# Attention scores in blocks of 64 by 64 in a fused attention and two-MLP kernel

## The chip, the cores and the metric

The kernel runs on one core of a Trainium2 chip. The metric is the device time of one execution in microseconds (us). Engines are named as in the profile: PE is TensorE's matrix multiply and PEld its weight loads, DVE is VectorE, ACT is ScalarE, POOL is GpSimd, and SP is the engine whose queue issues most DMA transfers.

## The reference, cut to what matters

Attention with decay over 2 batches, 8 heads, 768 positions and head dimension 64, in blocks of 64 positions, and then two MLPs on the 1536 rows of 512:

```python
for b in range(nb):                         # nb = 768 // 64 blocks
    intra = einsum('bhic,bhjc->bhij', qb, kb) * Dmask    # lam**(i-j) where i >= j, else 0
    intra = einsum('bhij,bhjd->bhid', intra, vb)
    inter = einsum('bhid,bhde->bhie', qb * lam_pow, kv_state)
    out[:, :, sl] = intra + inter
    kv_state = lam_block * kv_state + einsum('bhsd,bhse->bhde', kb * rev_pow, vb)
...
x = (h * cos(h)) @ w_out1      # h = x @ w_in1
y = (g * sigmoid(g)) @ w_out2  # g = x @ w_in2
```

Because the decay is a power of the distance, the kernel may use blocks of another length than 64: the result is the same.

## The kernel before, in words

All sequences of work are written out by hand: each engine runs its instructions in the order in which the program issues them, and waits on semaphores where its data come from another engine.

**Attention.** The kernel works in chunks of 128 positions, six of them (`SC = 6`), with both batches and all eight heads in one step. For a chunk it loads k, q and v (`load_qkv`, line 253, 512 KB each, on SP), transposes k and q on PE into PSUM (`transposed`, line 265, `pt`), and ACT copies the transposes to SBUF (`att_kT` line 269, `att_q` line 283). The PSUM tile of the k transposes and that of the q transposes share one buffer (tag "t", one buffer), so q's transposes wait until ACT has copied k's, and the next chunk's k transposes wait until ACT and DVE (`att_qdec`, line 291, `qd`) have read q's.

The scores of a chunk (`att_scores`, lines 335 to 344) are made in two calls, one per batch. A call has 8 products of 128 keys by 128 queries with a contraction of 64, two of which run at a time on the two row halves of the array. DVE then multiplies each of the two score tiles by the table `dm` of decay powers, in which the part above the diagonal is zero (line 344, 128 x 512). `att_inter` (line 357) adds the part from the running state: 16 products of 64 by 64 by 128, on the four quadrants of the array. `att_intra` (line 365) multiplies the masked scores by v: 16 products with a contraction of 128 keys, 64 output rows and 128 queries, on the two column halves. `att_kdec` and `att_kv` (lines 304 and 318) build the next state, `att_state` (lines 326 to 332) adds it to the decayed old one; the decay `sdec` of the new state is a POOL instruction (line 332). `att_x`, `att_t` and `att_l` (lines 377 to 410) turn the finished chunk into the operands of the first MLP: copies on ACT, differences `xt` on DVE (line 396), a rounding copy on ACT (line 408) and three subtractions on POOL (line 410), the third of which needs the copy of line 408.

**The order of a chunk.** Iteration `c` of the loop does `att_kv(c-1)`, `att_state(c-1)`, `att_scores(c-1, 0)`, `att_t(c-2)`, the k transposes of chunk `c`, `att_scores(c-1, 1)`, `att_kdec(c)`, `att_l(c-2)`, the q transposes of `c`, `att_inter(c-1)`, `att_qdec(c)`, `att_intra(c-1)`, `att_x(c-1)`. In iterations 3 and 4 there is also the preparation of the first weights of the MLP: `rebias_w` on ACT (line 112) before the copy of q's transposes, and `convert_w` on DVE (lines 121 and 122, `sb` and `w`) between `att_inter` and `att_qdec`. In iteration 5 there are also `sum_w` (line 143) and `split_plain` (lines 127 and 128).

**The start.** POOL makes the identity and the array `diag`. DVE makes the decay table by a scan along the free dimension (line 222, `dm<-step,diag`), a second scan makes the table `qp` (line 222). POOL copies one head's column of k and of q behind the last one (`head_17`, line 259), which the last transposes need.

**The end of the attention.** The last chunk's scores, `att_inter` and `att_intra` stand after the loop, between the first products of the first MLP (`product`, line 444). The MLP stages that follow (lines 440 to 750) are not touched.

Of the kernel before, what the change touches and what calls it, by code (L numbers as in the profile page):

```python
# [8 lines left out]
F32 = mybir.dt.float32  # L9
# [4 lines left out]
ALU = mybir.AluOpType  # L14
PSUM = bass.MemoryType.PSUM

P = 128
WARM = 4
TB = 512
HB = TB // 2  # L20
C = 64
# [19 lines left out]
def tile_decay_attention__two_mlps(  # L41
# [171 lines left out]
    def place(b, h):  # L213
        return (h - b) % H // 2, (h + b) % 2

    ident = ap_c.tile([P, P], F32, name="ident")
    lamb = ap_c.tile([P, P], F32, name="lamb")[:, 0:H + 1]
    dm = ap_c.tile([P, H + 1, P], F32, name="dm")
    qp = ap_c.tile([P, B, NP, P], F32, name="qp")

    def scan(out, step, first):
        nc.vector.tensor_tensor_scan(out=out, data0=step, data1=first, initial=0.0, op0=ALU.mult, op1=ALU.add)

    def table_dm():
        step = stage.tile([P, H, P], F32, tag="raw", name="step")
        nc.vector.tensor_copy(step, lamb[:, 0:H, None].to_broadcast([P, H, P]))
        nc.vector.memset(step[:, :, 0:1], 0.0)
        scan(*(t.rearrange("p h i -> p (h i)") for t in (dm[:, 0:H], step, diag)))
        nc.vector.tensor_copy(dm[:, H], dm[:, 0])

    def table_qp():
        first, step = both[:, 0], both[:, 1]
# [10 lines left out]
    def load_qkv(c, parts="kqv", engine=None):  # L243
        if c >= SC:
            return
        r = slice(c * P, (c + 1) * P)
        for part in parts:
            pool = ap_2 if part == "v" else ap_k
            t = pool.tile([P, 2 * H if part == "v" else 2 * H + 2, D], F32, tag=part, name=part, bufs=2 if part == "q" else 3)
            x = {"q": q, "k": k, "v": v}[part].rearrange("b h s d -> s (b h) d")[r]  # L250
            eng = engine or nc.sync
            for h in (slice(0, H), slice(H, 2 * H)) if c == 0 else (slice(0, 2 * H),):
                eng.dma_start(out=t[:, h], in_=x[:, h])
            qkv[c, part] = t
# [44 lines left out]
    def att_kdec(c):  # L299
        if c == SC - 1:  # L300
            return
        t = ap_k.tile([P, B, H, D], F32, tag="kd", name="kd", bufs=1)
        for b in range(B):
            (nc.gpsimd if c else nc.vector).tensor_tensor(
                out=t[:, b], in0=qkv[c, "k"][:, b * H:(b + 1) * H], in1=dm[:, 0:H, P - 1:P].to_broadcast([P, H, D]), op=ALU.mult
            )
        kd[c] = t

# [12 lines left out]
    def att_state(c):  # L321
        if c == SC - 1:
            return
        new = ap_2.tile([P, B, NP, D], F32, tag="state", name="state")
        if c:
            nc.vector.tensor_tensor(out=new, in0=pkv.pop(c), in1=sdec.pop(c), op=ALU.add)
        else:
            nc.vector.tensor_copy(new, pkv.pop(c))
        state[c + 1] = new
        if c < SC - 2:  # L330
            t = ap_2.tile([P, B, NP, D], F32, tag="sdec", name="sdec", bufs=1)
            nc.gpsimd.tensor_tensor(out=t, in0=new, in1=qp[:, :, :, P - 1:P].to_broadcast([P, B, NP, D]), op=ALU.mult)
            sdec[c + 1] = t

    def att_scores(c, b, pool, tag):
        (qT, _), kT = tr[c, "q"], tr[c, "k"]
        if b == 0:
            at[c] = ap_2.tile([P, B, 2, NP, P], F32, tag="at", name="at", bufs=1)
        ps = [pool.tile([P, NP, P], F32, tag=tag, name="psc", bufs=3) for _ in range(2)]
        for s in range(NP):  # L340
            for r in range(2):
                nc.tensor.matmul(ps[r][:, s, :], kT[half[r], b, s, :], qT[half[r], b, s, :], start=True, stop=True)  # L342
        for r in range(2):
            nc.vector.tensor_tensor(out=at[c][:, b, r], in0=ps[r], in1=dm[:, b + r:b + r + H - 1:2, :], op=ALU.mult)

    def att_inter(c, pool, tag):
        ps = pool.tile([P, B, NP, P], F32, tag=tag, name="pso")
# [5 lines left out]
        for s in range(NP):  # L353
            for e in range(2):
                for b in range(B):
                    u, r = place(b, 2 * s + e)
                    nc.tensor.matmul(ps[half[e], b, s, :], st[half[r], b, u, :], qd[half[r], b, u, :], start=s == 0, stop=False, skip_group_check=True)  # L357

    def att_intra(c):
        ps, a, vt = po[c], at.pop(c), qkv[c, "v"]  # L360
        for b in range(B):
            for s in range(NP):
                for e in range(2):
                    u, r = place(b, 2 * s + e)
                    nc.tensor.matmul(  # L365
                        ps[half[e], b, s, :], vt[:, b * H + 2 * s + e, :], a[:, b, r, u, :],
                        start=c == 0 and s == 0, stop=True, skip_group_check=True,
                    )

    def att_x(c):  # L370
# [473 lines left out]
    with tc.manual_schedule():  # L844
# [22 lines left out]
        nc.gpsimd.tensor_copy(diag, ident[:, None, :].to_broadcast([P, H, P]))  # L867
        both = ap_2.tile([P, 2, B, NP, P], F32, tag="at", name="both", bufs=1)
        nc.gpsimd.memset(both[:, 0], 0.0)
        nc.gpsimd.memset(both[:, 1, :, :, 0:1], 0.0)  # L870
        table_dm()

        for c in range(SC):
            if c == 0:
                pt = ps_t.tile([P, B, NP, P], F32, tag="t", name="pt")
                transposed(c, "k", pt, 0)
                warm(WARM)
                for part in "kq":
                    head_17(c, part, nc.gpsimd.tensor_copy)
                transposed(c, "k", pt, 1)  # L880
                att_kdec(c)
                table_qp()
                att_kT(c, pt)
                warm(WARM // 2)
                load_qkv(c + 2, "k")
                att_q(c, ps_o, "o")
                load_qkv(c + 2, "qv")
                head_17(c + 1, "k", nc.scalar.copy)
                continue
# [183 lines left out]
```

## Time and profile before

| what | value |
|---|---|
| median of 3 runs | 561.61 us (561.52 to 562.08) |
| time of the profiled execution | 561.36 us |
| its span in the trace | 559.5 us |
| PE busy | 553.3 us, 99% of the span |
| DVE, ACT, POOL busy | 357.4, 296.7, 185.2 us |
| chain that ended last | PE 96%, DVE 2%, DMA 1% |

Times inside the trace count from the start of the span. The profiled execution's own time is 1.86 us longer than its span, and 0.25 us below the median of the runs. A busy PE is not a PE at its peak, since matmuls are pipelined; what a piece of work costs on PE is read from the start of one group of matmuls to the start of the next.

### The profile page before, as it was taken

The numbers are of one execution on the slowest core, as the hardware profiler recorded it, in microseconds if no ns is written. First come the engines' busy times: TensorE is split into PE (matmuls) and PEld (weight loads), VectorE is DVE, ScalarE is ACT, GpSimd is POOL, SyncE is SP. The second block draws the span as 40 slices with busy tenths as digits, with TensorE's granted clock in tenths as the row PEclk, the third lists the DMA queues.
The fourth block names the chain that finished last, engine by engine and source line by source line (L and its number), as shares of the span: only waits on it lengthen the run. The fifth ranks groups of instructions, "written<-read, shape, count | busy, mean of one in ns | idle before, by whom it ended". The sixth has DMA issues, their size and how long they took to land.

```text
span 559.5 us, 8256 instructions
## 1 busy us (share of the span) xinstructions
PE 553.3 (99%) x3170; PEld 462.1 (83%) x3170; DVE 357.4 (64%) x452; ACT 296.7 (53%) x452; POOL 185.2 (33%) x162
## 2 busy tenths in 40 slices
PE   8999999999999999999999999999999999999997
PEld 5888788888888888888888898888888888888885
DVE  6697887777899976301896375666777966104322
ACT  5667577777788765202843575656656753101210
POOL 4699244444453000001552265555514000000000
PEclk9999999999999999999999999999999999999999
DMA  9994325554449988501322054455669993005501
GB/s 211 261 252 146 116 110 189 187 183 180 158 187 353 327 310 296 189 0 39 113 77 75 0 221 157 171 188 189 225 233 315 364 327 133 1 0 178 198 0 76
DMA packets 71032, 97.02 MB, mean 173 GB/s; under 512 B 40272, under 2 KB 40272, under 8 KB 70992
## 3 DMA queue, kind: packets, MB, share of 16 engines
q1 hardware_dynamic: 67680, 93.86, 49.6%
q10 hardware_dynamic: 3312, 2.63, 1.5%
q8 instruction: 25, 0.41, 0.3%
q14 instruction: 15, 0.12, 0.1%
HBM read 68.16 MB, written 28.31 MB: 172 GB/s over the span
## 4 chain that ended last, share of the span: by engine, by line
PE 96%; DVE 2%; DMA 1%; ACT 0%; POOL 0%; issue 0%; SPq 0%; DVEq 0%; ACTq 0%
PE cab L725 39%; PE cab L444 24%; PE d L444 10%; PE d L725 8%; PE cab L460 8%; PE psc L342 2%; PE pt L265 2%; PE pso L365 2%; DMA k<-in_k_dram 1%; PE pkv L318 1%; PE pso L357 1%; DVE S L143 1%; POOL k L259 0%; DVE sb L121 0%; DVE w L122 0%
## 5 line engine op out<-in xcount | busy, mean ns | idle before, releaser
L127 ACT CAST gh<-gf 128x512 fp32r<-128x512 f32 (+1 forms) x68 | 53.6, 796 | 89.9 <-DMA out_dram<-o 40.7
L725 PE MATMUL cab<-wout,gh 128*128 128x512 f32 x320 | 98.5, 389 | 0.0
L725 PE MATMUL cab<-gh,wout 128*128 128x512 f32 x320 | 98.4, 389 | 0.0
L444 PE MATMUL cab<-xah,win 128*128 128x512 f32 x320 | 86.8, 393 | 0.2 <-ACT u L481 0.2
L128 DVE TENSOR_TENSOR gl<-gf,gh 128x1024 fp32r<-128x1024 f32 (+1 forms) x46 | 46.5, 1014 | 46.7 <-ACT gh L127 23.9
L725 PEld LDWEIGHTS cab<-gh,wout 128*128 128x128 f32 x320 | 60.1, 188 | 12.4
L725 PEld LDWEIGHTS cab<-wout,gh 128*128 128x128 f32 x320 | 59.9, 188 | 12.3
L444 PEld LDWEIGHTS cab<-xah,win 128*128 128x128 f32 x320 | 58.9, 188 | 12.5 <-ACT u L481 0.7
L128 POOL TENSOR_TENSOR gl<-gf,gh 128x512 fp32r<-128x512 f32 x22 | 33.2, 1511 | 108.7 <-ACT gh L127 103.3
L725 PE MATMUL cab<-gl,wout 128*128 128x512 f32 x160 | 62.2, 389 | 0.0
L725 PE MATMUL cab<-wout,gl 128*128 128x512 f32 x160 | 62.2, 389 | 0.0
L143 POOL TENSOR_TENSOR S<-w 128x256 f32<-128x256 f32 x26 | 27.3, 1048 | 80.2 <-DVE w L122 80.2
L122 DVE SCALAR_TENSOR_TENSOR w<-w,sb 128x512 uint32<-128x512 uint32 x64 | 47.4, 740 | 4.8
L444 PE MATMUL cab<-xal,win 128*128 128x512 f32 x160 | 49.4, 390 | 0.0
L112 ACT ACTIVATE w<-raw 128x512 f32<-128x512 f32 x64 | 42.9, 672 | 1.0 <-DMA raw<-in_moe_w_out_dram 1.0
L481 ACT COPY u<-cab 128x512 f32<-128x512 f32 (+1 forms) x48 | 24.5, 511 | 30.6 <-PE cab L444 30.4
L519 DVE TENSOR_TENSOR s<-cab,s 128x1024 f32<-128x1024 f32 (+1 forms) x32 | 34.7, 1085 | 5.6 <-ACT s L513 3.7
L519 DVE TENSOR_TENSOR s<-h,s 128x1024 f32<-128x1024 f32 (+1 forms) x24 | 35.2, 1465 | 1.0 <-ACT s L513 0.7
L128 POOL TENSOR_TENSOR win<-w,win 128x512 fp32r<-128x512 f32 (+1 forms) x28 | 34.5, 1255 | 3.5 <-ACT win L127 3.5
L444 PEld LDWEIGHTS cab<-xal,win 128*128 128x128 f32 x160 | 30.0, 188 | 6.4
L725 PEld LDWEIGHTS cab<-wout,gl 128*128 128x128 f32 x160 | 30.0, 188 | 6.3
L725 PEld LDWEIGHTS cab<-gl,wout 128*128 128x128 f32 x160 | 30.0, 188 | 6.3
(134 smaller groups left out, 988.3 us busy)
## 6 DMA issues: line engine op xcount, KB each, us to landing
gf<-gd SPq DMA_DIRECT2D x45, 512.0 KB, 5.1
gd<-s SPq DMA_DIRECT2D x40, 512.0 KB, 2.9
raw<-in_moe_w_out_dram SPq DMA_DIRECT2D x32, 512.0 KB, 4.1
raw<-in_moe_w_in_dram SPq DMA_DIRECT2D x28, 512.0 KB, 4.0
gd<-s SPq DMA_DIRECT2D x16, 256.0 KB, 2.8
out_dram<-o SPq DMA_DIRECT2D x12, 256.0 KB, 2.1
k<-in_k_dram SPq DMA_DIRECT2D x5, 512.0 KB, 6.7
q<-in_q_dram SPq DMA_DIRECT2D x5, 512.0 KB, 6.5
```

The lines of the kernel that those rows point to most:

```text
L112: nc.scalar.activation(w, raw[piece][:, :, 1].bitcast(F32), AF.Prelu, scale=2.0**-112, alpha=-(2.0**32))
L122: nc.vector.scalar_tensor_tensor(out=w, in0=w, scalar=3, in1=sb, op0=ALU.logical_shift_left, op1=ALU.bitwise_or)
L127: nc.scalar.copy(hi, of)
L128: (engine or nc.gpsimd).tensor_tensor(out=lo, in0=of, in1=hi.bitcast(F32), op=ALU.subtract)
L143: engine.tensor_tensor(out=s[:, i], in0=x, in1=y, op=op)
L265: nc.tensor.transpose(pt[:, b, s, :], t[:, h:h + 2, :].rearrange("p h d -> p (h d)"), ident)
L342: nc.tensor.matmul(ps[r][:, s, :], kT[half[r], b, s, :], qT[half[r], b, s, :], start=True, stop=True)
L444: nc.tensor.matmul(Q.banks[bank], w[:, part, wu, kt * P:(kt + 1) * P], x[:, xu, kt, :], start=start and m == 0 and kt == 0, stop=m == 2 an ...
L460: nc.tensor.matmul(Q.cab[:, i], w[:, part, 2 * i + kt // 2, kt % 2 * P:(kt % 2 + 1) * P], x[:, kt, :], start=m == 0 and kt == 0, stop=m == ...
L481: nc.scalar.copy(t, Q.banks["b"])
L519: nc.vector.tensor_tensor(out=t, in0=source(Q, i), in1=t, op=ALU.mult)
L725: nc.tensor.matmul(y[m], x, z, start=f == 0 and n == 0, stop=f == FT - 1 and n == 2)
```

## The change

The scores of a chunk are kept as three blocks of 64 queries per head pair instead of four: the block in which all keys lie behind the queries, which the mask clears, is neither computed nor multiplied by v. To lay the three blocks out evenly over the partitions, the second batch's k and v are loaded with the two halves of 64 positions swapped. The core of the diff:

```diff
-    dm = ap_c.tile([P, H + 1, P], F32, name="dm")
+    dm = ap_c.tile([P, 2, NP, 3, C], F32, name="dm")
+    kdec = consts[:, 16:16 + B * H].rearrange("p (b h) -> p b h", b=B)
...
-        scan(*(t.rearrange("p h i -> p (h i)") for t in (dm[:, 0:H], step, diag)))
-        nc.vector.tensor_copy(dm[:, H], dm[:, 0])
+        scan(*(t.rearrange("p h i -> p (h i)") for t in (powers[:, 0:H], step, diag)))
+        for e in range(2):
+            for b in range(B):
+                nc.vector.tensor_copy(kdec[half[e], b], powers[half[e], 0:H, P - 1 if e == b else C - 1])
+        nc.vector.tensor_copy(powers[:, H], powers[:, 0])
+
+    def table_blocks(copy, *which):
+        for e, b, cols, blocks in which:
+            copy(
+                dm[half[e]].rearrange("p r s m c -> p r s (m c)")[:, :, :, blocks],
+                powers[half[e], b:b + H, cols].rearrange("p (s r) i -> p r s i", r=2),
+            )
...
-            for h in (slice(0, H), slice(H, 2 * H)) if c == 0 else (slice(0, 2 * H),):
-                eng.dma_start(out=t[:, h], in_=x[:, h])
+            if part == "q":
+                for h in (slice(0, H), slice(H, 2 * H)) if c == 0 else (slice(0, 2 * H),):
+                    eng.dma_start(out=t[:, h], in_=x[:, h])
+            else:
+                eng.dma_start(out=t[:, 0:H], in_=x[:, 0:H])
+                for e in range(2):
+                    eng.dma_start(out=t[half[e], H:2 * H], in_=x[half[1 - e], H:2 * H])
...
+    def att_sdec(c):
         if c < SC - 2:
             t = ap_2.tile([P, B, NP, D], F32, tag="sdec", name="sdec", bufs=1)
-            nc.gpsimd.tensor_tensor(out=t, in0=new, in1=qp[:, :, :, P - 1:P].to_broadcast([P, B, NP, D]), op=ALU.mult)
+            (nc.vector if c else nc.gpsimd).tensor_tensor(
+                out=t, in0=state[c + 1], in1=qp[:, :, :, P - 1:P].to_broadcast([P, B, NP, D]), op=ALU.mult
+            )
...
-        for s in range(NP):
-            for r in range(2):
-                nc.tensor.matmul(ps[r][:, s, :], kT[half[r], b, s, :], qT[half[r], b, s, :], start=True, stop=True)
+        for i in range(2):
+            s = 2 * n + i
+            for second in range(2):
+                for b in range(B):
+                    e = b ^ second
+                    blocks = slice(1 + b, 2 + b) if second else slice(0, 2 + b, 1 + b)
+                    for r in range(2):
+                        nc.tensor.matmul(
+                            ps[r][half[e], i, blocks], kT[half[r], b, s, half[e]],
+                            qT[half[r], b, s, second * C:].rearrange("p (m c) -> p m c", c=C), start=True, stop=True,
+                        )
         for r in range(2):
-            nc.vector.tensor_tensor(out=at[c][:, b, r], in0=ps[r], in1=dm[:, b + r:b + r + H - 1:2, :], op=ALU.mult)
+            u = slice(2 * n, 2 * n + 2)
+            nc.vector.tensor_tensor(out=at[c][:, r, u], in0=ps[r], in1=dm[:, r, u], op=ALU.mult)
...
+        nc.scalar.copy(consts[C:C + 1, 4:5], ps[C:C + 1, B - 1, NP - 1, 0:1])
...
-                        ps[half[e], b, s, :], vt[:, b * H + 2 * s + e, :], a[:, b, r, u, :],
+                        ps[half[e], b, s, C:], vt[:, b * H + 2 * s + e, :], a[:, r, u, 1 + b],
                         start=c == 0 and s == 0, stop=True, skip_group_check=True,
                     )
+        for s in reversed(range(NP)):
+            for e in (1, 0):
+                for b in (1, 0):
+                    u, r = place(b, 2 * s + e)
+                    nc.tensor.matmul(
+                        ps[half[e], b, s, 0:C], vt[half[b], b * H + 2 * s + e, :], a[half[b], r, u, 0],
+                        start=False, stop=True, skip_group_check=True,
+                    )
...
+                c1, c2 = slice(0, C), slice(C, 2 * C)
+                table_blocks(nc.gpsimd.tensor_copy, (1, 1, c1, c1), (1, 0, c1, c2), (0, 1, c1, slice(2 * C, 3 * C)), (1, 1, c2, slice(2 * C, 3 * C)))
...
                 att_q(c, ps_o, "o")
+                table_blocks(nc.scalar.copy, (0, 0, slice(0, P), slice(0, P)))
...
             att_scores(c - 1, 1, ps_s, "s")
+            att_sdec(c - 1)
```

`att_kdec` multiplies by `kdec` instead of a column of `dm`. `diag` has its ones in both halves' first 64 columns, made by a POOL memset and a POOL addition of half the size instead of one copy. The one-element copy on ACT (`nc.scalar.copy(consts...)`) is the last line of `att_inter`; it reads PSUM that the second group of products in `att_intra` writes. `att_sdec` is called behind the second call of the scores, where before it was the end of `att_state`.

## Rows read from the trace of the kernel before

**Rows 1.** Stages (start:end, length, engines' busy us, clock, DMA share), 9 to 45 us by queue.
```profile
33.60:41.77 8.17, 8.16 (x148) 7.27 (x146) 7.16 (x12) 5.78 (x9) 7.98 (x7) 1.00 1.12 277
...
63.56:559.50 495.94, 492.16 (x2322) 412.90 (x2322) 309.08 (x382) 258.45 (x388) 138.59 (x117) 1.00 0.47 169
...
q1 hardware_dynamic: 30951, 8.12, 99.2%
```

**Rows 2.** Timeline of PE: start us, us, what, idle before; the start, then iteration 4.
```profile
9.97 1.15 PE L318 MATMUL pkv<-v,kd 128*64 128x64 f32 x32
...
14.43 1.09 PE L265 MATMUL pt<-ident,q 128*128 128x128 f32 x8
...
33.60 1.10 PE L318 MATMUL pkv<-v,kd 128*64 128x64 f32 x32
34.63 1.16 PE L342 MATMUL psc<-qT,kT 64*128 64x128 f32 x16
35.72 1.09 PE L265 MATMUL pt<-ident,k 128*128 128x128 f32 x8
...
37.92 1.09 PE L265 MATMUL pt<-ident,q 128*128 128x128 f32 x8
38.94 1.10 PE L357 MATMUL pso<-qd,state 64*64 64x128 f32 x32
39.98 1.97 PE L365 MATMUL pso<-at,v 128*64 128x128 f32 x32
```

**Rows 3.** Timeline of ACT in iteration 4.
```profile
36.85 1.01 ACT L269 COPY kT<-pt 128x1024 f32<-128x1024 f32 x1 [0.86 <-PE pt L265]
...
38.66 1.06 ACT L408 CAST xah<-xt 128x1024 fp32r<-128x1024 f32 x1 [0.65 <-DVE xt L396]
39.61 0.69 ACT L112 ACTIVATE w<-raw 128x512 f32<-128x512 f32 x1
40.20 1.00 ACT L283 COPY qT<-pt 128x1024 f32<-128x1024 f32 x1
```

**Rows 4.** Timeline of DVE and POOL in the start.
```profile
5.80 2.29 DVE L222 TENSOR_TENSOR_SCAN dm<-step,diag 128x1024 f32<-128x1024 f32 x1
...
8.27 1.29 DVE L304 TENSOR_TENSOR kd<-k,dm 128x512 f32<-128x512 f32 x2
...
12.34 1.29 DVE L344 TENSOR_TENSOR at<-psc,dm 128x512 f32<-128x512 f32 x2
...
6.57 1.56 POOL L259 COPY k<-k 128x64 f32<-128x64 f32 x1 [3.22 <-DMA k<-in_k_dram]
8.92 0.73 POOL L259 COPY q<-q 128x64 f32<-128x64 f32 x1 [0.80 <-DMA q<-in_q_dram]
```

**Rows 5.** Timeline of DVE and POOL in iteration 4.
```profile
37.74 0.88 DVE L396 TENSOR_TENSOR xt<-pso,xt 128x256 f32<-128x256 f32 x2
...
40.33 1.03 DVE L122 SCALAR_TENSOR_TENSOR w<-w,sb 128x512 uint32<-128x512 uint32 x1
41.28 1.21 DVE L291 TENSOR_TENSOR qd<-pt,qp 128x1024 f32<-128x1024 f32 x1
...
35.59 1.06 POOL L332 TENSOR_TENSOR sdec<-state,qp 128x512 f32<-128x512 f32 x1 [0.19 <-DVE state L326]
...
38.64 2.17 POOL L410 TENSOR_TENSOR xal<-xc,xah 128x512 fp32r<-128x512 f32 x2
40.77 2.82 POOL L410 TENSOR_TENSOR xal<-xt,xah 128x1024 fp32r<-128x1024 f32 x1
```

**Rows 6.** Groups by line and shape: count, busy us, mean ns, idle before.
```profile
L344 DVE TENSOR_TENSOR at<-psc,dm 128x512 f32<-128x512 f32 x24 | 15.4, 684 | 3.4 <-PE psc L342 3.4
...
L122 DVE SCALAR_TENSOR_TENSOR w<-w,sb 128x512 uint32<-128x512 uint32 x14 | 10.4, 740 | 0.9
...
L396 DVE TENSOR_TENSOR xt<-pso,xt 128x256 f32<-128x256 f32 x8 | 3.4, 425 | 0.3
...
L867 POOL COPY diag<-ident 128x1024 f32<-128x1024 f32 x1 | 1.0, 1037 | 0.1
```

**Rows 7.** Timeline of PE where the first MLP takes over.
```profile
63.56 1.19 PE L444 MATMUL cab<-xah,win 128*128 128x512 f32 x4 [0.22 <-ACT u L481]
```

More of the change, by code (lines that the diff above doesn't have):

```diff
@@ L227, in table_dm @@
         nc.vector.memset(step[:, :, 0:1], 0.0)
-        scan(*(t.rearrange("p h i -> p (h i)") for t in (dm[:, 0:H], step, diag)))
-        nc.vector.tensor_copy(dm[:, H], dm[:, 0])
+        scan(*(t.rearrange("p h i -> p (h i)") for t in (powers[:, 0:H], step, diag)))
[9 more added lines that the diff above has]
+            )
     def table_qp():
-        first, step = both[:, 0], both[:, 1]
         nc.scalar.copy(lamb[:, H:], lamb[:, 0:1])
@@ L304, in att_kdec @@
             (nc.gpsimd if c else nc.vector).tensor_tensor(
-                out=t[:, b], in0=qkv[c, "k"][:, b * H:(b + 1) * H], in1=dm[:, 0:H, P - 1:P].to_broadcast([P, H, D]), op=ALU.mult
+                out=t[:, b], in0=qkv[c, "k"][:, b * H:(b + 1) * H], in1=kdec[:, b, :, None].to_broadcast([P, H, D]), op=ALU.mult
             )
@@ L329, in att_state, with att_scores @@
         state[c + 1] = new
+    def att_sdec(c):
         if c < SC - 2:
             t = ap_2.tile([P, B, NP, D], F32, tag="sdec", name="sdec", bufs=1)
-            nc.gpsimd.tensor_tensor(out=t, in0=new, in1=qp[:, :, :, P - 1:P].to_broadcast([P, B, NP, D]), op=ALU.mult)
+            (nc.vector if c else nc.gpsimd).tensor_tensor(
+                out=t, in0=state[c + 1], in1=qp[:, :, :, P - 1:P].to_broadcast([P, B, NP, D]), op=ALU.mult
+            )
             sdec[c + 1] = t
-    def att_scores(c, b, pool, tag):
+    def att_scores(c, n, pool, tag):
         (qT, _), kT = tr[c, "q"], tr[c, "k"]
-        if b == 0:
-            at[c] = ap_2.tile([P, B, 2, NP, P], F32, tag="at", name="at", bufs=1)
-        ps = [pool.tile([P, NP, P], F32, tag=tag, name="psc", bufs=3) for _ in range(2)]
-        for s in range(NP):
-            for r in range(2):
-                nc.tensor.matmul(ps[r][:, s, :], kT[half[r], b, s, :], qT[half[r], b, s, :], start=True, stop=True)
+        if n == 0:
+            at[c] = ap_2.tile([P, 2, NP, 3, C], F32, tag="at", name="at", bufs=1)
+        ps = [
+            pool.tile([P, TB], F32, tag=tag, name="psc", bufs=3)[:, 0:2 * 3 * C].rearrange("p (s m c) -> p s m c", s=2, c=C)
+            for _ in range(2)
+        ]
+        for i in range(2):
[9 more added lines that the diff above has]
+                        )
         for r in range(2):
-            nc.vector.tensor_tensor(out=at[c][:, b, r], in0=ps[r], in1=dm[:, b + r:b + r + H - 1:2, :], op=ALU.mult)
+            u = slice(2 * n, 2 * n + 2)
+            nc.vector.tensor_tensor(out=at[c][:, r, u], in0=ps[r], in1=dm[:, r, u], op=ALU.mult)
     def att_inter(c, pool, tag):
@@ L866, in tile_decay_attention__two_mlps @@
         diag = stage.tile([P, H, P], F32, tag="raw", name="diag")
[L867 to L870, printed above, removed]
+        nc.gpsimd.memset(diag[:, :, C:], 0.0)
+        nc.gpsimd.tensor_tensor(
+            out=diag[:, :, 0:C], in0=ident[:, None, 0:C].to_broadcast([P, H, C]),
+            in1=ident[:, None, C:].to_broadcast([P, H, C]), op=ALU.add,
+        )
+        powers = ap_2.tile([P, 2 * NP * 3 * C], F32, tag="at", name="powers", bufs=1)[:, 0:(H + 1) * P].rearrange(
+            "p (h i) -> p h i", i=P
+        )
+        first, step = (ap_2.tile([P, B, NP, P], F32, tag=t, name=t, bufs=1) for t in ("xc", "xt"))
+        nc.gpsimd.memset(first, 0.0)
+        nc.gpsimd.memset(step[:, :, :, 0:1], 0.0)
         table_dm()
```

## The prediction

> **What bounds the kernel now.** I read the stage table first. In an iteration of the attention loop PE is busy for 8.16 of 8.17 us, and from 63.56 us to the end for 492 of 496 us; the change touches only what lies before 63.56 us [rows 1]. So the question is by how much 63.56 moves: what follows is PE's own work and moves with it. The timeline of PE gives what each step costs, from the start of one group to that of the next [rows 2]. The other engines' timelines show which step on PE is really a wait [rows 3 to 5]. Times below are for iteration 4, counted from the start of its `pkv` at 33.60.
>
> **PE, step by step.** Four matmuls run at once where contraction and output are 64 wide, two where only one is. `pso` of line 357, 16 products by quadrants on 128 columns, takes 1.03 us (38.94 to 39.98); line 365, 16 products by column halves on 128 columns, 1.79 (39.98 to 41.77); `pkv`, the same by 64 columns, 1.03 [rows 1, 2]. The pair on 64 columns is thus cheaper by (1.79 - 1.03)/16 = 0.048 us than on 128.
> - A call of the scores was 1.09. It becomes, by quadrants, 4 groups on 128 columns and 4 on 64: 1.03 - 4 x 0.048 = 0.84, so 0.25 less.
> - Line 365 becomes 16 products by column halves on 64 columns (1.03) and 16 by quadrants on 64 (1.03 - 8 x 0.048 = 0.65): 1.68 against 1.79.
> - The shape of the array changes twice more per chunk. `pkv` after transposes takes 1.15, after line 365, which has its shape, 1.10 [rows 2]: 0.05 each.
> - The second call of the scores gives nothing. The q transposes start at 37.92, 0.05 after ACT has ended the copy of k's, 36.85 to 37.87 [rows 2, 3], and must wait for their shared buffer; those 2.20 from 35.72 stay.
>
> In all 0.25 + 0.11 - 0.10, about 0.3 with rounding, per iteration: four iterations from 17.25 us on give **-1.2**.
>
> **The start.** The mask table now takes five copies, four of them on POOL, before the first masked scores, and a lock gets in their way. POOL's copy of a 64-wide column took 1.56 us and ended at 8.13, when DVE's scan, 5.80 to 8.09, ended; the next took 0.73 and ended at 9.65, behind DVE's `kd` (to 9.56) [rows 4]. A POOL instruction stands still while DVE reads two operands from SBUF. In the new order DVE does four small copies (some 0.06 each, an estimate), `kd` and the second scan, 2.29 like the first, until about 12.1; only then do POOL's copies run. At 1.04 us for 1024 elements [rows 6] four copies of 512 take 2.1 to 2.2: the table is ready at 14.3, where the first product with it used to start at 12.34 [rows 4]. The second call of the scores needs that product's PSUM buffer; it starts at 14.9, and q's transposes at 15.7 instead of 14.43 [rows 2]. **+1.2**. Bounds: 0 if POOL is not held up, +1.8 if a copy costs 0.7. I take the middle since both POOL copies in the rows ended with DVE's instruction.
>
> **sdec, moved.** POOL loses 1.06 per iteration [rows 5], so its subtractions of line 410 come earlier, and DVE gains a product with two SBUF operands: 0.65, as each `kd` [rows 4]. DVE's score products shrink from 512 to 384 columns: between 425 ns for 256 and 684 for 512 [rows 6], 0.55. `xt` ended at 38.62 [rows 5], that is 5.02; it comes 0.45 earlier, at 4.57. `sdec` then runs from 5.45 to 6.1. POOL is ahead of it by now and waits for the copy of line 408, 1.06 from the end of `xt` [rows 3]: its long subtraction (2.82, of it 0.4 or so waiting for `w`) asks for the port at 5.7, before DVE's `sb` and `w` of iterations 3 and 4 ask, at 6.0. Whoever asks first goes first: `w` asked at 40.33, while POOL's short ones ran to 40.81, and took 1.03 where its mean is 0.74; POOL's long one, which asked at 40.77, then waited for it [rows 5, 6]. So now the long one runs from 6.1 to 8.45, `sb` and `w` end at 9.5, `qd` (1.21, [rows 5]) at 10.65. The next k transposes want `qd`'s buffer at 9.8 and get it at 10.65: 0.85 late, of which I count 0.75 since later DVE work is late too. Twice: **+1.5**. This is the page "SBUF — State Buffer" of the Trainium skill too, section "Who interferes with whom": an exclusive lock for whole instructions, by order of issue. If instead DVE always went first, this term would be 0.
>
> **The new copy on ACT.** The second group of line 365's products waits for it. It stands behind `qT` (1.00), in iterations 3 and 4 behind line 112 (0.69) as well, and those behind line 408 and `xt` [rows 3]. With `xt` at 4.57 ACT gets to it at 7.1 to 7.3, and PE is there at 7.25: free. But where DVE is late by the term above, `xt` ends at 5.8, ACT at 8.5, PE at 8.05: 0.45. In iteration 5 ACT has two copies for the first weights more, so 0.5 again. **+0.95**. Alone, without the late DVE, this costs 0 to 0.6, in iteration 5.
>
> **Loads.** k and v go as three transfers instead of one, two of them of 64 partitions. Their number of 256-byte pieces is the same, and SP has time. The queue was 99% busy from 9 to 45 us, at 277 GB/s in iteration 4 [rows 1]: there is no room for a slower transfer. No row shows one of 64 partitions. Bounds: 0, and twice the time for a third of the bytes, 0.5 MB at 277 GB/s or 1.9 us per iteration. I take 0, the same pieces on the same queue. The Trainium skill ("SBUF — State Buffer", "Door 1: The DMA port swizzle") says that a transfer of 64 partitions reaches half the ports, and gives 196 against 328 GB/s; by that it would be an estimated 1.1 us per iteration.
>
> **After the loop.** At 63.56 PE waits for ACT's `u` by 0.22 us [rows 7]: a chain of DVE, POOL and ACT sets that point, so PE's savings there are hidden, and the shorter scores before the chain give back some **-0.35**.
>
> **Sum.** -1.2 + 1.2 + 1.5 + 0.95 - 0.35 = +2.1. On the profiled execution's 561.36 (1.86 over its span of 559.5, and 0.25 under the median) that is 563.45; against the median **563.7 us**. A measurement of this kernel tells 0.2%, 1.1 us, from no change.
>
> **Rivals.**
> - *No lock where I put it* (faster, 0.15). POOL's copies fit in before DVE's second scan and the long subtraction falls behind `w`. Then the start costs nothing and the saving on PE stays: -1.2 - 0.35 and up to 0.3 for an earlier start of the second call, 559.8 to 560.3. For it: POOL is then free when it matters, and an order that differs by 0.3 us (5.7 against 6.0) decides. Against it: two copies held up by DVE in rows 4.
> - *The lock in the start alone* (0.23). `sb` and `w` go before the long subtraction: if it asks after 6.7 instead of 5.7 they do. +1.2 - 1.2 - 0.35 and 0.6 for the ACT copy of iteration 5: 561.9, no change.
> - *Loads of half the partitions are slower* (0.12). The rule above, as a mechanism of this kernel: q and k of iterations 2 and 3 land late and PE's transposes wait for them. q of iteration 3 was the closest. From 0.3 us more per k or v load the loop goes by the loads; at 0.6 I get +4 to +5, 566, with the start's delay hidden under it.
> - *No four at a time on 64 columns* (0.07). The groups of 64 by 64 by 64 then cost as much as on 128 columns: 8 x 0.048 more in line 365, 0.2 in the first call, per iteration 0.6 for four or five, less what the waits above hide: +3.4, 565. The quadrant rows are all on 128 columns, so nothing excludes it.
>
> **How the numbers follow.** My forecast has 0.43, as both terms of the lock are needed for it. Slower by over 0.2% takes it and the last two rivals, 0.43 + 0.12 + 0.07 = 0.62; within 0.2% the start alone, 0.23; faster the first, 0.15. The range goes from 560.4, which leaves most of the first rival out, to 567.0, where the loads at 0.6 us are in and worse is out. The likeliest case's own range is 562.6 to 564.8, from the start's 0.3 to 1.8 and the ACT copy's 0.5 to 1.0.
>
> **What would show it.** Right: POOL's four copies in the start end near 14.3, the first being over 2 us long; DVE's `sb` in iterations 3 and 4 over 2 us long; k transposes of iterations 4 and 5 that wait for `qd`; scores by 0.84 and line 365 in two parts of 1.05 and 0.65. Wrong: q transposes that start sooner than 2.2 us after k's, transposes that wait for DMA, or PE at the first MLP's `u` wait earlier than 63.56.

## The result, and the profile after

Measured beside each other, the changed kernel took 567.61 us (567.18 to 569.12, five runs) and the kernel before 562.07: a ratio of 1.0109, with an interval of 1.0098 to 1.0120. (The ratio is not that of the two medians, which differ by 5.5 us.) By the ratio the change costs about 6.1 us where 2.1 were forecast, and the time lies 0.6 above the forecast's range. Its profiled execution took 567.61 too, 1.8 over its span.

The stage table says first where it went (start:end, length, busy us and instructions of PE, PEld, DVE, ACT and POOL, clock, DMA share, GB/s; first iteration 4, then from the start of the first MLP's product at line 491 to the end).

```profile
37.77:47.43 9.66, 8.11 (x214) 6.85 (x209) 8.69 (x13) 6.14 (x10) 6.37 (x5) 1.00 0.99 228
69.79:565.80 496.01, 492.18 (x2323) 412.88 (x2322) 308.46 (x382) 258.58 (x388) 141.10 (x117) 1.00 0.48 169
```

SP's queue from 9 to 45 us, in the view of the DMA queues (packets, MB, share of 16 engines):

```profile
q1 hardware_dynamic: 26333, 6.62, 81.8%
```

Against [rows 1]: the last stage is as long as before (496.01 against 495.94), at a full clock, so everything happened ahead of it, where 63.56 became 69.79. An iteration takes 9.66 instead of 8.17 with about the same busy time of PE, 8.11; the queue that was 99.2% busy is down to 81.8%.

PE's timeline in iterations 4 and 5 and at its other long waits (as [rows 2]: start, length, what, idle before it and who ended that):

```profile
15.77 1.09 PE L285 MATMUL pt<-ident,q 128*128 128x128 f32 x8
...
18.50 1.15 PE L338 MATMUL pkv<-v,kd 128*64 128x64 f32 x32
19.58 0.90 PE L375 MATMUL psc<-qT,kT 64*64 64x128 f32 x32
20.41 1.09 PE L285 MATMUL pt<-ident,k 128*128 128x128 f32 x8
...
23.90 1.06 PE L285 MATMUL pt<-ident,q 128*128 128x128 f32 x8 [1.57 <-DMA q<-in_q_dram]
...
40.64 0.63 PE L285 MATMUL pt<-ident,k 128*128 128x128 f32 x4 [0.31 <-DMA k<-in_k_dram]
41.20 0.90 PE L375 MATMUL psc<-qT,kT 64*64 64x128 f32 x29
43.07 0.33 PE L375 MATMUL psc<-qT,kT 64*64 64x64 f32 x3 [0.97 <-issue]
43.33 1.09 PE L285 MATMUL pt<-ident,q 128*128 128x128 f32 x8
44.35 1.10 PE L394 MATMUL pso<-qd,state 64*64 64x128 f32 x32
45.72 1.15 PE L404 MATMUL pso<-at,v 128*64 128x64 f32 x32 [0.27 <-ACT consts L396]
46.80 0.69 PE L412 MATMUL pso<-at,v 64*64 64x64 f32 x32
47.43 1.29 PE L338 MATMUL pkv<-v,kd 128*64 128x64 f32 x32
...
55.84 1.15 PE L404 MATMUL pso<-at,v 128*64 128x64 f32 x32 [2.04 <-ACT consts L396]
...
57.44 0.85 PE L375 MATMUL psc<-qT,kT 64*64 64x128 f32 x32
...
69.79 1.19 PE L491 MATMUL cab<-xah,win 128*128 128x512 f32 x4
```

And PE's waits from 9 to 75 us, summed (us in total, times, longest):

```profile
PE pso L404 <- ACT consts L396: 3.2, 4, 2.0
PE pt L285 <- DMA q<-in_q_dram: 1.6, 1, 1.6
PE psc L375 <- issue: 1.2, 2, 1.0
PE pt L285 <- DMA k<-in_k_dram: 0.9, 2, 0.6
```

Before, PE had one wait in that stretch, 0.22 for `u` [rows 7]. Two more lines of the kernel before mark where its four iterations begin and end:

```profile
17.25 1.10 PE L318 MATMUL pkv<-v,kd 128*64 128x64 f32 x32
...
50.05 1.16 PE L342 MATMUL psc<-qT,kT 64*128 64x128 f32 x16
```

Three differences add up to the 6.23 by which that point moved. The second `pkv` starts at 18.50 instead of 17.25: +1.25. The four iterations from there to the last chunk's scores at 57.44 take 38.94 instead of 32.80: +6.14. From there to 69.79 it is 12.35 instead of 13.51: -1.16, and the wait for `u` is gone, since the chain behind it is now ready first. In the iterations the rows hold 2.45 of waits for q and k, 3.2 for the small ACT copy and 1.2 of gaps inside the scores that no event explains; less the forecast saving of 1.2 that is 5.65 of the 6.14, and some 0.5 stays unassigned.

The start is as long as foreseen: POOL's table copies run from 9.12 to 14.31, beside DVE's `kd` and second scan. They do not wait for the scan's end, though: the first two take 0.96 and 1.07 beside `kd`, the third 2.51 beside the scan, the last 0.61.

```profile
10.54 2.70 DVE L228 TENSOR_TENSOR_SCAN qp<-xt,xc 128x1024 f32<-128x1024 f32 x1
...
14.34 1.02 DVE L381 TENSOR_TENSOR at<-psc,dm 128x384 f32<-128x384 f32 x2 [0.52 <-POOL dm L242]
...
8.63 0.24 POOL L279 COPY k<-k 128x64 f32<-128x64 f32 x1 [4.68 <-DMA k<-in_k_dram]
...
9.12 5.19 POOL L242 COPY dm<-powers 64x512 f32<-64x512 f32 x4
```

In iterations 3 and 4 one step of DVE each is over 2 us long, beside POOL's long subtractions of 34.50 to 37.30 and 43.73 to 46.09:

```profile
35.01 2.58 DVE L121 TENSOR_SCALAR sb<-raw 128x512 uint32<-128x512 uint32 x1
...
44.31 2.33 DVE L354 TENSOR_TENSOR sdec<-state,qp 128x512 f32<-128x512 f32 x1
```

The longest wait, 2.04 us in iteration 5, is read on ACT, which does the copy behind `qT` and behind line 112, which itself waited for a late weight load:

```profile
53.65 1.01 ACT L303 COPY qT<-pt 128x1024 f32<-128x1024 f32 x1
54.94 0.68 ACT L112 ACTIVATE w<-raw 128x512 f32<-128x512 f32 x1 [0.28 <-DMA raw<-in_moe_w_in_dram]
55.64 0.15 ACT L396 COPY consts<-pso 1x1 f32<-1x1 f32 x1
```

### The profile page after: what moved, and what is told of

It is laid out like the page before. It is cut to its first block, busy times and chain, and to the rows that moved or that the text cites. A ratio compares the mean times of both kernels' runs of the same rounds, so it can differ in the third digit from the quotient of the medians.

```text
span 565.8 us, 9087 instructions
## 1 busy us (share of the span) xinstructions
PE 551.5 (97%) x3554; PEld 459.3 (81%) x3554; DVE 359.8 (64%) x459; ACT 299.2 (53%) x458; POOL 187.5 (33%) x164
## 4 chain that ended last, share of the span: by engine, by line
PE 91%; SPq 4%; DMA 3%; issue 1%; ACT 1%; DVE 0%; ACTq 0%
PE cab L772 38%; PE cab L491 24%; PE d L491 10%; PE d L772 8%; PE cab L507 8%; SPq L273 2%; SPq L271 1%; DMA q<-in_q_dram 1%; DMA k<-in_k_dram 1%; DMA raw<-in_moe_w_in_dram 1%; PE pso L404 1%; PE psc L375 1%; PE pso L394 1%; PE pt L285 0%; PE pso L412 0%
## 5 line engine op out<-in xcount | busy, mean ns | idle before, releaser
L128 POOL TENSOR_TENSOR gl<-gf,gh 128x512 fp32r<-128x512 f32 x22 | 34.7, 1579 | 106.9 <-ACT gh L127 102.5
L143 POOL TENSOR_TENSOR S<-w 128x256 f32<-128x256 f32 x26 | 27.3, 1049 | 81.8 <-DVE w L122 81.8
L122 DVE SCALAR_TENSOR_TENSOR w<-w,sb 128x512 uint32<-128x512 uint32 x64 | 44.7, 698 | 4.8
```

The source lines that it names most:

```text
L122: nc.vector.scalar_tensor_tensor(out=w, in0=w, scalar=3, in1=sb, op0=ALU.logical_shift_left, op1=ALU.bitwise_or)
L128: (engine or nc.gpsimd).tensor_tensor(out=lo, in0=of, in1=hi.bitcast(F32), op=ALU.subtract)
L143: engine.tensor_tensor(out=s[:, i], in0=x, in1=y, op=op)
```

## The experiments

Two theories stood at the outset: **Loads** (more transfers, two of them of 64 partitions, land later, and PE waits for q and k) and **Fence** (PE waits for the small ACT copy of line 396 between the products of the state, line 394, and those with v). Each ratio is to runs of the kernel before measured beside it.

**1. Loads undone alone, copy moved alone.** Whole loads:

```diff
-                eng.dma_start(out=t[:, 0:H], in_=x[:, 0:H])
-                for e in range(2):
-                    eng.dma_start(out=t[half[e], H:2 * H], in_=x[half[1 - e], H:2 * H])
+            for h in (slice(0, H), slice(H, 2 * H)) if c == 0 else (slice(0, 2 * H),):
+                eng.dma_start(out=t[:, h], in_=x[:, h])
```

> The changed kernel with k and v loaded in one transfer each, as before; the heads of the second batch then lie unswapped, so the kernel multiplies by the wrong halves of k and v there, with the same instructions and sizes. Theory Loads (the transfers land later than before, and PE waits for q and k by 1.57, 0.57 and 0.31 us in iterations 2 to 4): those 2.45 us go, the queue's rate is back at about 257 GB/s from 9 to 45 us, and the fence copy of iteration 5 is no longer behind a wait for a DMA: 564.0 to 565.2. Theory Fence (all of the loss in the loop is PE waiting for the small ACT copy between the two groups of products): PE, no longer late, waits for that copy instead: 566.5 to 567.6.

Measured: 564.89, ratio 1.0056 (1.0044 to 1.0068), about 3.0 us less than the whole change and within the range given for Loads. The queue is at 93.3%, and PE waits for no load in the loop, but not all is won:

```profile
PE pso L399 <- ACT consts L391: 4.0, 4, 1.6
PE psc L370 <- DVE at L376: 1.4, 1, 1.4
PE pt L280 <- ACT q L274: 0.8, 1, 0.8
```

PE is earlier, and the copy (L391 here) now costs 4.0 instead of 3.2. The 1.4 lies in the start, where the change has 0.84. The early copy:

```diff
-            att_q(c, ps_t, "t")
+            att_q(c, ps_t, "t", lambda: att_inter(c - 1, ps_o, "o"))
...
-            att_inter(c - 1, ps_o, "o")
```

where `att_q` calls the function it is given behind its transposes and ahead of its copy.

> The changed kernel with the products of the state, and the small ACT copy behind them, issued ahead of ACT's copy of the transposed q instead of behind it. Theory Fence: the waits of PE for that copy, 0.27, 0.63, 0.27 and 2.04 us, 3.2 in all, go: 564.2 to 565.0. Theory Loads: PE gains the 2.04 of iteration 5 at most and in the others waits for k and q instead: 565.5 to 566.5. If the copy matters to nothing: 567.6.

Measured: 564.50, ratio 1.0053 (1.0034 to 1.0071), about 3.1 less and within the range given for Fence. In its profile the wait for the copy is down to 1.1 in all, 0.27 each time; the waits for k and q in the loop stay, 2.7 against 2.45. Both causes are there: each edit alone takes off about 3 us and leaves the other's waits.

**2. Both together.**

> Both of the edits that helped alone, together: k and v in one transfer each (so the second batch's halves lie unswapped and the kernel multiplies by the wrong halves there, with the same instructions and sizes), and the products of the state with the small ACT copy ahead of ACT's copy of q. In the run with whole loads alone the four gaps ahead of the line after the copy were 0.84, 1.39, 0.92 and 1.92 us, where 0.2 is the normal step; early, each was 0.54. If the two causes are all of it and add up: 4.26 - 1.36 = 2.9 less than with whole loads alone, 562.0, and no wait for q or k over 0.3. If another wait takes their place (DVE's product with q held up by its own earlier work): 563 to 564.9, with k's transposes waiting for DVE.

Measured: 563.89, ratio 1.0039 (1.0026 to 1.0053), so the rival came nearer: of the 2.9 expected beyond whole loads about 1.0 came (1.0056 to 1.0039). The two edits together take off 3.9 of the change's 6.1, though one by one they take off 3.0 and 3.1, so each cost hides part of the other. Part of the loss is a wait for `u`: the four iterations are 2.0 shorter than with whole loads alone (34.26 against 36.23), but from there to the first MLP's sums it takes 0.95 longer (13.34 against 12.39), with PE waiting 0.84 for `u` again. In iterations 4 and 5 a wait that the prediction had named, and that the changed kernel did not show, appears:

```profile
37.16 1.09 PE L280 MATMUL pt<-ident,k 128*128 128x128 f32 x8 [0.41 <-DVE qd L308]
...
46.17 1.09 PE L280 MATMUL pt<-ident,k 128*128 128x128 f32 x8 [0.45 <-DVE qd L308]
```

Then with the products of the state between the two batches of q's transposes, and two table copies on ACT:

> As the run before it, with two things more: the products of the state stand between the transposes of q's first and second batch, so PE has work while ACT does the small copy; and two of POOL's four copies of the mask table go to ACT, where it is idle. Theory: 1.36 for the copy's own time goes, less 0.1 to 0.4 for more changes of the array's shape, and the start gains 0.9 (table ready at 13.3 instead of 14.31): 560.0 to 560.6, faster than before. If the start is hidden by loads that are no earlier: 560.9 to 561.5. If PE waits for DVE's or ACT's later copies of q instead: 562 or more.

Measured: 563.00, ratio 1.0024 (1.0014 to 1.0035). The wait for the copy is gone from the list, but q's transposes wait 1.4 for a load, and 1.0 that the list puts down to ACT's column copy of q, which had ended 0.7 before. The gain that the theory gave did not come; the time lies in the range of the third case, and PE waits only in part for what that case named.

**3. The start, and the moved product, each undone in the changed kernel.** The start:

```diff
-                table_blocks(nc.gpsimd.tensor_copy, (1, 1, c1, c1), (1, 0, c1, c2), (0, 1, c1, slice(2 * C, 3 * C)), (1, 1, c2, slice(2 * C, 3 * C)))
+                table_blocks(nc.gpsimd.tensor_copy, (1, 1, c1, c1), (0, 1, c1, slice(2 * C, 3 * C)))
...
+                table_blocks(nc.scalar.copy, (1, 0, c1, c2))
                 att_kT(c, pt)
...
-                table_blocks(nc.scalar.copy, (0, 0, slice(0, P), slice(0, P)))
+                table_blocks(nc.scalar.copy, (0, 0, slice(0, P), slice(0, P)), (1, 1, c2, slice(2 * C, 3 * C)))
```

> The changed kernel with only the start edited: two of POOL's four copies of the mask table go to ACT. Table ready at 13.3 instead of 14.31 and the q transposes of iteration 1 at 14.9 instead of 15.77. If the start's delay is paid to the end, as the prediction had it: 0.9 less than the changed kernel, 566.7. If the late loads hide it (q of iteration 1 landed at 14.85, q of iteration 2 at 23.77): no change, 567.6.

Measured: 567.06, ratio 1.0096 (1.0078 to 1.0115). That interval holds both cases, so the time cannot tell 0.9 less from no change. PE's timeline shows this:

```profile
15.22 1.09 PE L285 MATMUL pt<-ident,q 128*128 128x128 f32 x8
...
17.95 1.15 PE L338 MATMUL pkv<-v,kd 128*64 128x64 f32 x32
...
22.59 0.63 PE L285 MATMUL pt<-ident,k 128*128 128x128 f32 x4 [2.07 <-DMA k<-in_k_dram]
```

The start gains 0.55, not the 0.9 expected (second `pkv` at 17.95 instead of 18.50), and iteration 2 then waits 2.07 for k, where the change waits 1.57 for q. The sdec product back on POOL:

```diff
-            (nc.vector if c else nc.gpsimd).tensor_tensor(
+            nc.gpsimd.tensor_tensor(
                 out=t, in0=state[c + 1], in1=qp[:, :, :, P - 1:P].to_broadcast([P, B, NP, D]), op=ALU.mult
```

> The changed kernel with the product of the state with its decay back on POOL, at its new place. The prediction gave the move to DVE 1.5 us through the lock that it shares with POOL. If that holds: 566.1 or so. If the late loads and the small ACT copy set the pace and DVE's delays lie beside them: 567.3 to 567.9, no change. If POOL is now late with its subtractions: above 568.

Measured: 568.07, ratio 1.0114 (1.0088 to 1.0141): no difference from 1.0109, and the interval begins above the 566.1 of the first case.

**4. Each suspect alone, added to the kernel before.** There PE waits for nothing but 0.22 for `u`, so a cost shows undisturbed. The copy:

```diff
+        nc.scalar.copy(consts[C:C + 1, 4:5], ps[C:C + 1, B - 1, NP - 1, 0:1])
```

behind the loop of line 357.

> The kernel before with nothing but the small ACT copy added, between the products of the state and those with v: one element that nobody reads. Theory Fence: in iterations 2 to 5 the products with v wait as in the changed kernel with whole loads, where the four gaps were together 4.26 us over the normal step: 564.6 to 566.0. The prediction's own figure for it, alone: 0 to 0.6, 561.6 to 562.2.

Measured: 566.47, ratio 1.0082 (1.0070 to 1.0095): 4.6 us for a copy of one element. Here it is line 358, and the products with v are line 366:

```profile
24.35 1.97 PE L366 MATMUL pso<-at,v 128*64 128x128 f32 x32 [0.80 <-ACT consts L358]
...
33.96 1.97 PE L366 MATMUL pso<-at,v 128*64 128x128 f32 x32 [1.37 <-ACT consts L358]
```

The four waits sum to 5.2. The sdec product alone, moved to DVE behind the second call of the scores:

```diff
-            nc.gpsimd.tensor_tensor(out=t, in0=new, in1=qp[:, :, :, P - 1:P].to_broadcast([P, B, NP, D]), op=ALU.mult)
+            (nc.vector if c else nc.gpsimd).tensor_tensor(out=t, in0=state[c + 1], in1=qp[:, :, :, P - 1:P].to_broadcast([P, B, NP, D]), op=ALU.mult)
...
             att_scores(c - 1, 1, ps_s, "s")
+            att_sdec(c - 1)
```

> The kernel before with nothing but the product of the state with its decay moved from POOL to DVE, at the place that it has in the change. The prediction's lock term: k's transposes of iterations 4 and 5 wait for DVE's product with q, 1.5 us in all: 562.8 to 563.4. If DVE's long step falls beside other work: 561.4 to 561.8.

Measured: 564.15, ratio 1.0039 (1.0027 to 1.0051), 2.2 us. The timelines of PE, DVE and POOL in iteration 3:

```profile
37.67 1.09 PE L265 MATMUL pt<-ident,k 128*128 128x128 f32 x8 [1.85 <-DVE qd L291]
...
32.18 2.59 DVE L121 TENSOR_SCALAR sb<-raw 128x512 uint32<-128x512 uint32 x1
34.88 1.60 DVE L122 SCALAR_TENSOR_TENSOR w<-w,sb 128x512 uint32<-128x512 uint32 x1
36.40 1.21 DVE L291 TENSOR_TENSOR qd<-pt,qp 128x1024 f32<-128x1024 f32 x1
...
31.63 2.86 POOL L412 TENSOR_TENSOR xal<-xt,xah 128x1024 fp32r<-128x1024 f32 x1 [0.93 <-ACT xah L410]
```

`sdec` pushes `sb` behind the start of POOL's long subtraction; `sb`, 0.41 us at its shortest after the change, takes 2.59 and ends soon after POOL does; `qd` and k's transposes are late, by 1.85 here and 1.21 in the next iteration. Put back on POOL in the run with whole loads and the early copy:

> The run with whole loads and the early copy, with the product of the state with its decay back on POOL. There k's transposes of iterations 4 and 5 waited 0.48 and 0.52 us for DVE's product with q, behind a step of DVE of over 2 us. If that comes from the moved product: those waits go, 562.6 to 563.2. If it comes from POOL's long subtraction wherever that product stands, or the chain up to the first MLP's sums takes it back: 563.6 to 564.2.

Measured: 563.29, ratio 1.0028 (1.0018 to 1.0038), against 1.0039 with it on DVE: the intervals overlap, but the two waits for `qd` are gone from the profile, so the moved product made them. In their place q's transposes of iteration 4 wait 1.4; the list puts that down to ACT's column copy of q, which had ended 1.0 before, and q had landed well ahead, so what ended it is not shown.

**5. Number or shape of the transfers.** All in the kernel before. Split in three by rows, as in the change but unswapped:

```diff
+                eng.dma_start(out=t[:, 0:H], in_=x[:, 0:H])
+                for e in range(2):
+                    eng.dma_start(out=t[half[e], H:2 * H], in_=x[half[e], H:2 * H])
```

> The kernel before, k and v as three transfers instead of one: the first batch on 128 partitions, the second as two of 64 partitions (not swapped, so nothing else differs). If it is the number of transfers or the half partitions that makes loads late: slower than before by 1.5 to 3 us, 563.1 to 564.6, with PE waiting for k and q. If the loads go as before: 561.6 to 562.0.

Split in three by heads, each of 128 partitions:

```diff
+                for h in (slice(0, H), slice(H, H + H // 2), slice(H + H // 2, 2 * H)):
+                    eng.dma_start(out=t[:, h], in_=x[:, h])
```

> The kernel before, k and v as three transfers of the same sizes as in the change, but each of all 128 partitions. If the number of transfers counts (each waits on its queue for an earlier one to land, so more and smaller ones keep less under way): slower like the split by rows, within 0.6 us of it, and the same stops of SP at the loads. If transfers of 64 partitions are slower by themselves: 561.6 to 562.0, as before.

Measured: by rows 564.10, ratio 1.0042 (1.0029 to 1.0056); by heads 562.65, ratio 1.0012 (1.0003 to 1.0021). Both cost, rows more. With shape and number taken apart, the next three runs load k and v in two transfers by rows (`out=t[half[e], 0:2 * H]` for each half), in two by heads and in four by heads:

> The kernel before, k and v in two transfers each of 64 partitions and all 16 heads: 5 transfers per chunk, and all bytes of k and v in transfers of half the partitions. If half the partitions is what costs: more than the split in three with two thirds of the transfers so (1.0042), 564 to 566. If only the number counts: between one transfer each (561.9) and three (562.7 to 564.1), 562.0 to 562.8, and the same as the split by heads beside it.

> The kernel before, k and v in two transfers each of 8 heads and all 128 partitions: the number and size of the run beside it. If the number counts: 562.0 to 562.8. If only half the partitions count: as before, 561.9.

> The kernel before, k and v in four transfers each of 4 heads and all 128 partitions, 9 per chunk. If the number of transfers counts: more than with three (1.0012), 563 to 565, with a lower rate of the queue from 9 to 45 us than the 87.8% of three. If only half the partitions count: as before, 561.9.

Measured: two by rows 563.73, ratio 1.0038 (1.0026 to 1.0050); two by heads 562.17, 1.0007 (0.9998 to 1.0016); four by heads 563.93, 1.0043 (1.0030 to 1.0056), with the queue at 88.6%, not below the 87.8% of three. Two by rows lies between its two ranges, and two by heads can't be told from before. By time alone shape and number both count. The timelines show where. With two by rows, PE's timeline:

```profile
7.60 0.63 PE L269 MATMUL pt<-ident,k 128*128 128x128 f32 x4 [2.12 <-DMA k<-in_k_dram]
...
19.72 0.46 PE L322 MATMUL pkv<-v,kd 128*64 128x64 f32 x10
```

And its stages (columns as in the first table; the last is the four iterations):

```profile
6.00:8.00 2.00, 0.40 (x4) 0.43 (x5) 1.83 (x3) 0.56 (x2) 0.41 (x1) 1.00 1.29 272
8.00:10.00 2.00, 2.00 (x11) 1.34 (x9) 2.00 (x3) 0.00 (x0) 0.98 (x2) 0.65 1.31 240
10.00:12.00 2.00, 2.00 (x9) 1.47 (x8) 1.13 (x1) 1.01 (x1) 0.00 (x0) 0.50 1.11 218
...
19.72:52.51 32.79, 32.73 (x580) 29.03 (x576) 26.29 (x41) 23.55 (x37) 29.41 (x25) 1.00 0.94 241
```

Its whole loss is in the start: the first k transposes begin at 7.60, where two by heads begin at 5.30, since each half carries both batches and both halves are needed; the granted clock then falls to 0.50, which is 1.2 GHz, after PE was busy for 0.40 of 2 us, so part of the loss is the clock's (q's transposes take 1.50 to the next group, 0.97 in two by heads); and the second `pkv` comes at 19.72 instead of 17.25. The four iterations take 32.79, as before (32.80), with no wait for a load; the loop runs 2.5 us later, though, which would hide loads late by as much. Three by rows lose 0.8 in the start, where the second batch's k transposes begin at 8.64 with a wait of 0.98 for the load, against 6.93 and 7.35 for three by heads. They lose 1.7 in the loop (18.05 to 52.59); four by heads lose 2.0 in the loop (17.12 to 51.92) and nothing in the start. So in the loop the number is enough to make loads late, and in the start the shape; whether the shape counts in the loop too is not settled. Three by heads lost 2.5 in the loop of their profiled execution, the slowest of eleven, while by the ratio they are 0.7 over before.

**6. What is left of the change.** The best that keeps all of its work:

> The changed kernel, loads untouched, with the products of the state and the small ACT copy early, and two of POOL's copies of the mask table on ACT. If the start is hidden by late loads, as when it was edited alone: 564.2 to 564.8, as with the early copy alone. If it now counts: 563.6 to 564.0. Either way slower than before, since the loads are untouched.

Measured: 564.45, ratio 1.0040 (1.0028 to 1.0052), as expected, and still slower than before. And with all four side costs cut:

> The changed kernel with all four side costs cut: k and v in one transfer each (so the second batch's halves lie unswapped and the kernel multiplies by the wrong halves there, with the same instructions), the small ACT copy early, the moved product back on POOL, two of the table's copies on ACT. What is left of the change is PE's saving of 1.2 and the small copy's own 0.34 per iteration, 1.36: 561.7 to 562.3, no difference from before. If the start or late loads still count: 562.6 to 563.3, as with three of the four.

Measured: 562.34, ratio 1.0013 (1.0003 to 1.0022), 0.7 us slower than before. The profiled execution, whose timeline of PE follows, is the fastest of twelve (561.26), so it does not hold those 0.7:

```profile
17.47 1.15 PE L335 MATMUL pkv<-v,kd 128*64 128x64 f32 x32
...
40.40 1.15 PE L401 MATMUL pso<-at,v 128*64 128x64 f32 x32 [0.27 <-ACT consts L393]
...
50.21 0.85 PE L372 MATMUL psc<-qT,kT 64*64 64x128 f32 x32
...
63.52 1.19 PE L488 MATMUL cab<-xah,win 128*128 128x512 f32 x4 [0.80 <-ACT u L525]
```

The four iterations take 32.74 against 32.80. PE's own steps have become 1.4 us shorter (1.2 forecast), and the copy, early and behind nothing, makes the step after the state's products 0.54 instead of 0.20 in each of four iterations, 1.36. The shorter work after the loop ends in a wait of 0.80 for `u`, so that 63.56 becomes 63.52. Against the run with whole loads, the early copy and the product on POOL (1.0028) only the start differs: it gains 0.55 in the rows (17.47 against 18.02), and the time about 0.8, with intervals that just overlap. No version beat the kernel before. The place of the copy between the two batches of q's transposes, where the list shows no wait for it, was not tried with the product back on POOL. The change without the copy was not tried: the products of line 394 and of line 412 write the same buffers from different halves of the rows. The Trainium skill ("PSUM — Partial Sum Buffer", "PSUM bank collisions raise a hardware error") leaves it to the program to keep such products apart in time; no run here shows what happens otherwise.

## Why the prediction was wrong

Slower was right, the size was not: +2.1 forecast, +6.1 measured.

- **PE's own steps: right.** A call of the scores takes 0.83 (19.58 to 20.41; forecast 0.84), the products with v 1.08 and 0.63 (forecast 1.05 and 0.65), so four products do run at once on 64 columns. The saving is in the timeline, 1.4 over the four iterations where nothing else is late, and the second call of the scores gave nothing, as said. But the copy that the change needs eats it even ahead of ACT's other work (section 6).
- **Loads: the first step that failed.** "I take 0, the same pieces on the same queue." PE waits 2.45 for them in the loop, which the prediction itself had named as a sign that it was wrong, and undoing them alone takes off 3.0. The pieces are the same, but there are seven transfers per chunk instead of three. In the kernel before, seven by rows cost 2.4, seven by heads 0.7 and nine by heads 2.4: the number alone can cost that much, and at seven the shape adds to it. The rival on loads named the place ("q and k of iterations 2 and 3 land late") and gave 566; its cause, half the partitions, is shown in the start alone, where with three by rows the two halves of the second batch's k landed at 7.01 and 8.51, and with three by heads the same bytes at 5.93 and 7.30. One packet of 256 bytes did not take longer: SP's queue was busy for 89.6% of 16 times 36 us for 28275 packets with two transfers by rows, 18.3 ns each, 17.9 by heads (95.0%, 30589) and 18.5 before [rows 1]. The Trainium skill ("SBUF — State Buffer", "Door 1: The DMA port swizzle") gives 196 against 328 GB/s for 64 and 128 partitions at 1 MiB; neither the packets nor the iterations of that run show it, and the later k of the start may have another cause.
- **Why more transfers land later: open.** In the program each DMA also waits for the landing of the one whose semaphore it takes, most often eight before it. By the trace of the changed kernel that one had landed ahead of every issue, also at v's first transfer, where SP stands for 2.4 to 5 us per iteration (landed at 25.06, issue from 26.09 to 31.05), so that wait is not what holds SP there. What the issue and landing times in the traces do show is that less is under way on SP's queue, on average from 9 to 45 us, counted from the end of a transfer's issue to its landing: 1013 KB before, 836, 767 and 680 with two, three and four by heads, 746 in the changed kernel.
- **The ACT copy: the second step that failed.** "The second group of line 365's products waits for it ... PE is there at 7.25: free." In the trace the first group (line 404) waits already, as it writes the buffer that ACT reads, though not the element; PE is there 1.1 us sooner, and has nothing else to do. Instead of 0.95 the waits were 3.2, and 5.2 in the kernel before with nothing but the copy. With the copy at 7.1 to 7.3, as the prediction had it, and PE at 6.2, the same rows gave about 1 per iteration. With whole loads the copy stood at 7.3 and 7.2 in iterations 3 and 4, so its time was right, and the instruction that waits for it was taken for a later one.
- **The lock: right as a mechanism, without effect here.** Alone in the kernel before the moved product costs 2.2, by the chain that was forecast (`sb` 2.59, `w` 1.60, late `qd`, k's transposes that wait 1.85 and 1.21). In the changed kernel `sb` is 2.58 long at 35.01, in iteration 4 `sdec` instead (2.33 at 44.31, with `sb` at 0.41), but PE comes later itself, for loads and the copy, and no k transposes wait for `qd`: the term of 1.5 measured 0, and back on POOL, nothing changes that the runs can tell. The Trainium skill ("SBUF — State Buffer", "Who interferes with whom") calls this an exclusive lock; `sb` of 2.58 beside a subtraction of 2.80, and 0.41 without one, agrees with it.
- **The start: right in size, not in what it is worth.** +1.2 forecast, 1.25 seen (table ready at 14.31, q's transposes at 15.77; forecast 14.3 and 15.7). The way there was not the one forecast: two copies ran beside `kd`, at about 1.0 each instead of some 0.5, and only the third stood beside the scan, 2.51, so the close sum is in part luck. The second batch's k, which lands later in the change, is not the reason: with whole loads POOL's copy of its column starts at 6.40 instead of 8.63, yet the table copies end at 14.20 and q's transposes start at 15.67. Whether the delay is paid at the end depends on what else is late: 0.55 of it taken back is followed by a longer wait for k in the changed kernel, and shows in the time where the other costs are gone (section 6).
- **After the loop:** -0.35 forecast, -1.16 seen, since late PE finds the chain for `u` ready.
- **The sum** took terms as if they added up. Alone the copy costs 4.6, the transfers by rows 2.4 and the moved product 2.2, 9.2 together before the start; with the saving of 1.2 the whole change costs 6.1. Where PE waits for one late thing, the others catch up.

## What to carry to other kernels

Where an engine is busy for 99% of a stage, an edit that gives it less work is judged by what it must wait for: for each wait that is added, find the first instruction that touches the buffer, not the one that needs the value, and the place of the releasing instruction in its own engine's order. A wait for a copy of 0.15 us cost 4.6 us behind other work and 1.4 ahead of it, as much as the change saved. Splitting a load into three or more cost time here although bytes and packets stayed the same, so measure number and shape of transfers each alone; and price several delays of one engine together, by which comes last, not as a sum.

## What was unexpected on the chip

- Splitting k's and v's loads from one transfer into two, three and four by heads, with the same packets, gave 1.0007, 1.0012 and 1.0043.
- Inside the changed kernel's scores PE stood still twice, 0.22 at 30.07 and 0.97 at 43.07, with nothing in the profile that ends it. Three more runs with the change's loads (the start edited, the product back on POOL, early copy and start) show such gaps of 0.7 to 1.1 in all, the early copy alone one of 0.2. The runs with whole loads show none inside the scores; but three of them have a wait of 0.8 to 1.4 right behind, ahead of q's transposes of iteration 4, put down to a column copy that had ended 0.5 to 1.0 before. The cause is open.
- In the kernel with two transfers by rows TensorE was granted 0.50 of its clock from 10 to 12 us, after a slice in which it was busy for 0.40 of 2 us.
